# Moving the decoding of weight half-chunks between the stages of an attention and mixture-of-experts kernel

## The chip, the core and the metric

The kernel runs on one core of one Trainium2 chip. The metric is device time in microseconds (us); lower is better. The engines are TensorE (PE in the rows, its weight loads PEld), VectorE (DVE), ScalarE (ACT), GpSimd (POOL) and SyncE (SP), which here only issues DMAs. Each engine takes its instructions in the order in which the program gives them.

## The reference

```python
# 8 batches x 8 heads x 576 positions x 64: causal decayed attention without softmax
attn = ((q @ k.T) / 8 * gamma**(i - j) * (i >= j)) @ v
x = attn as (4608 tokens, 512)
# routing: the 36864 logits x @ w_gate in falling order; a token goes to the first
# of its experts that still has room (576 tokens for each of 8 experts)
for e in range(8):
    out[mask_e] = relu(x[mask_e] @ w1[e]) @ w2[e]        # 512 -> 1024 -> 512
h = out @ w_in                                           # 512 -> 2048
return (h * sigmoid(1.702 * h)) @ w_out                  # 2048 -> 512
```

The weights `w_in` and `w_out` of the last layer come as double precision numbers (8 bytes each), the others as 4-byte floats.

## The kernel before

**Stages.** `build` first runs attention, in 40 iterations (8 batches times 5 blocks of positions). In each it loads blocks ahead, multiplies on TensorE, and puts logits, routing counts and row transposes from the list `fills` in between. Then `R.phase(0, True)` finds the tokens of the first expert, and `ffn` runs the rest. There, `gather(0)` fetches the first expert's 576 rows by five indirect DMAs that GpSimd issues; `prepare` transposes them on TensorE and splits them into a high part `xh` (ScalarE) and a low part `xl` (VectorE), because every product is made of three matmuls (`mm3`). Eight rounds follow. A round is `expert(k)` (w1, then w2, 192 matmuls each) and `block(k)` (the last layer for 512 tokens, 384 matmuls); a ninth block ends the program.

**Decoding.** `w_in` and `w_out` are 16 chunks of 128x1024, and each is decoded in two halves, so there are 32 half-chunks, numbered i. `decode_steps` gives six steps for one of them: s0 loads 512 KB (tile `draw`, SP); s1 is two ScalarE operations (`dr`, `dT`); s2 is two VectorE operations on `dT`; s3 one on VectorE (`dq`); s4 is one VectorE operation, a GpSimd multiplication into `dr` and a GpSimd addition into `dq`; s5 writes `dq` to the array `w32` in DRAM (SP). Blocks read their weights from `w32` later (L456). Before, half-chunks 0 to 17 are decoded in attention, number i at iteration int(2.1 i), with the steps 0, 3, 3, 4, 4 and 6 iterations after it (`AOFF`), and 18 to 31 in the first round.

**Order in the first round.** The program order inside `ffn` is written by a counter of ticks. `tick()` is called after each pair or single of `mm3` groups; it issues what the dictionary `timed` holds for this tick and then one step of the generator `follow(k + 1)`, which does the routing of the next expert (VectorE comparisons `ind`, then counting matmuls on TensorE, line L236 and so on), its gather and its `prepare`. `expert` takes 65 ticks and `block` 128. A half-chunk that starts at tick t has its steps at t + 0, 8, 10, 11, 12 and 14 (`OFF`); number 18 starts at tick 0 and each next one `DSTEP` = 10 ticks later. Because the counting matmuls stand between the block's matmuls in TensorE's queue, they hold TensorE when their `ind` is late.

**Buffers and queues.** In `ffn` a half-chunk uses tiles of the pool `fp` with `FDB` = (2, 2, 1, 2) buffers for `draw`, `dr`, `dT` and `dq`: there is one `dT` buffer, which is free again after the GpSimd multiplication. In attention each has 3. Weight chunks are loaded by `load_to` (SP, tile `raw`, 3 buffers) and split by `split_to` into `wh` (ScalarE) and `wl` (GpSimd or VectorE).

**The start of `ffn`** (L651 to L664):

```python
    warm(WU[0])                  # 9 matmuls without use
    xg = gather(0)
    split_to(2, nc.vector)       # w1 chunks 0 and 1: loads, wh, wl
    load_to(LD)                  # loads of w1 chunks 2 and 3
    rest = prepare(0, xg, True)
    next(rest)
    warm(WU[1])                  # 3 matmuls
    for _ in range(3):
        next(rest)
    for i in range(NDEC, 32):
        for f, o in zip(decode_steps(nc, fp, A, w32, i, 1, nc.vector), OFF):
            timed.setdefault(DSTEP * (i - NDEC) + o, []).append(f)
```

`expert(0)` then takes the transposes of row groups 2, 3 and 4 before its first, second and third matmul group, and asks for the split of w1 chunk 2 before its first group.

Of the kernel before, what the change touches and what calls it, by code (L numbers as in the profile page):

```python
# [25 lines left out]
BIG = 1.5e38  # L26
DEAD = -1.4e38
LAG = 2
NATT, NDEC, DFAST, DSTEP = 18, 18, 14, 10
OFF = (0, 8, 10, 11, 12, 14)  # L30
AOFF = (0, 3, 3, 4, 4, 6)
GD, DB = 1, 3
# [1 line left out]
FDB = (2, 2, 1, 2)  # L34
SL, GW, SW, YW = 1, 8, 2, 1
LGA = 1
X0, XS, XRB = 0, 2.1, 3
PF, XB, GDEF = 5, 3, 30
WU = (9, 3)
AJ = 0  # L40
# [347 lines left out]
def ffn(tc, ctx, A, out, R, xd, w32, idn):  # L388
    nc = tc.nc
    fa = ctx.enter_context(tc.tile_pool(name="first", bufs=1))  # L390
    fp = ctx.enter_context(tc.tile_pool(name="ffn", bufs=1))
# [5 lines left out]
    def gather(k):  # L397
        gi = R.GI[k]
        xg = []
        for g in range(5):  # L400
            w = 128 if g < 4 else 64
            x = fa.tile([128, DM], FT, name="xg", bufs=5)
            nc.gpsimd.indirect_dma_start(out=x[:w], out_offset=None, in_=xd[:],
                                         in_offset=bass.IndirectOffsetOnAxis(ap=gi[:w, g:g + 1], axis=0))
            xg.append(x)
        return xg
# [39 lines left out]
    def load_to(n):  # L446
        while ptr[0] < min(n, len(stream)):
            i = ptr[0]
            kind, k, j = stream[i]
            r = fa.tile([128, 1024], FT, name="raw", bufs=3)  # L450
            if kind[1] in "12":
                if k not in RV:
                    RV[k] = nc.sync.value_load(EI[k][0:1, 0:1], min_val=0, max_val=E - 1)
                nc.sync.dma_start(r, A[kind][ds(RV[k], 1), j].rearrange("e p f -> (e p) f"))
            else:
                nc.sync.dma_start(r, w32[(0 if kind == "wi" else 8) + j])  # L456
            RAW[i] = r
            ptr[0] += 1

    def split_to(n, eng_=None, wait=0):  # L460
        while ptr[1] < min(n, len(stream)):
            i = ptr[1]
            load_to(i + 1)
            r = RAW.pop(i)
            h = fa.tile([128, 1024], FR, name="wh", bufs=4)
            l = fa.tile([128, 1024], FR, name="wl", bufs=4)
            eng = eng_ or nc.gpsimd if stream[i][0] in ("w1", "wi") else nc.vector
            for a in (slice(0, 512), slice(512, 1024)):
                nc.scalar.activation(h[:, a], r[:, a], AF.Copy)  # L469
                f = partial(eng.tensor_tensor, l[:, a], r[:, a], h.bitcast(FT)[:, a], op=OP.subtract)  # L470
                later(wait, f) if wait else f()
            HL[i] = (h, l)
            ptr[1] += 1
# [16 lines left out]
    timed = {}  # L490
    now = [0]

    def later(n, f):
        timed.setdefault(now[0] + n, []).append(f)
# [151 lines left out]
    def warm(n):  # L646
        ps = pp.tile([128, 512], FT, name="po3")
        for _ in range(n):
            nc.tensor.matmul(ps, R.grp, R.zz.rearrange("p a b -> p (a b)"), start=True, stop=True)

    warm(WU[0])  # L651
    xg = gather(0)
    split_to(2, nc.vector)
    if GT is not None:
        nc.sync.dma_start(spacer2, xg[GT][:1, :1])
    load_to(LD)
# [2 lines left out]
    warm(WU[1])  # L659
    for _ in range(3):  # L660
        next(rest)
    for i in range(NDEC, 32):
        for f, o in zip(decode_steps(nc, fp, A, w32, i, 1, nc.vector), OFF):
            timed.setdefault(DSTEP * (i - NDEC) + o, []).append(f)  # L664
    for k in range(E):
        if k + 1 < E:
            gens.append(follow(k + 1))
# [7 lines left out]
def decode_steps(nc, pool, A, w32, i, bufs, eng):  # L675
    j, hf = divmod(i, 2)
    src = A["wi"][j] if j < 8 else A["wo"][j - 8]
    st = {}

    def s0():  # L680
        st["raw"] = pool.tile([128, 512, 2], I32, name="draw", bufs=DB if bufs > 2 else FDB[0])
        nc.sync.dma_start(st["raw"].rearrange("p a b -> p (a b)"), src[:, hf * 512:(hf + 1) * 512].bitcast(I32))

    def s1():
        raw = st["raw"]
        st["r"] = r = pool.tile([128, 512], FT, name="dr", bufs=bufs if bufs > 2 else FDB[1])
        st["T"] = T = pool.tile([128, 512], I32, name="dT", bufs=bufs if bufs > 2 else FDB[2])
        nc.scalar.activation(r, raw[:, :, 0].bitcast(U32), AF.Copy, scale=2.0 ** -52)
        nc.scalar.activation(T.bitcast(FT), raw[:, :, 1].bitcast(FT), AF.Abs)

    def s2():
        T = st["T"]
        nc.vector.tensor_scalar(T.bitcast(FT), T.bitcast(FT), LEAST, None, op0=OP.max)
        nc.vector.tensor_scalar(T, T, 3, 0x3FFFFFF8, op0=OP.logical_shift_left, op1=OP.bitwise_and)

    def s3():
        st["q"] = q = pool.tile([128, 512], FT, name="dq", bufs=bufs if bufs > 2 else FDB[3])
        nc.vector.scalar_tensor_tensor(q.bitcast(I32), st["raw"][:, :, 1], -0x40000000, st["T"], op0=OP.bitwise_and,
                                       op1=OP.bitwise_or)

    def s4():
        q, r, T = st["q"], st["r"], st["T"]
        nc.vector.tensor_scalar(T, q.bitcast(I32), -0x800000, None, op0=OP.bitwise_and)
        nc.gpsimd.tensor_mul(r, r, T.bitcast(FT))
        nc.gpsimd.tensor_add(q, q, r)

    def s5():
        nc.sync.dma_start(w32[j][:, hf * 512:(hf + 1) * 512], st["q"])
    return [s0, s1, s2, s3, s4, s5]


def build(tc, A, out, dbg=None, stop=None):
    nc = tc.nc
# [7 lines left out]
    w32 = dram.tile([16, 128, 1024], FT, name="w32")  # L721
    L = cp.tile([128, NCOL, 8], FT, name="L")
    idn = cp.tile([128, 128], FT, name="idn")
    with ExitStack() as ac:
# [156 lines left out]
        for i in range(NDEC):  # L881
            st = decode_steps(nc, al, A, w32, i, 3, nc.vector)
            if i < NATT:
                x = int(X0 + XS * i)
                for f, o in zip(st, AOFF):
                    sched.setdefault(min(x + o, NCH - 1), []).append(f)
            else:
                sched.setdefault(NCH - 1, []).append(st[0])
                extra.append(st[1:])
# [60 lines left out]
    if dbg and "SI" in dbg:  # L950
        for k in range(1, E):
            for _ in R.phase(k):
                pass
        nc.sync.dma_start(dbg["L"], L)
        nc.sync.dma_start(dbg["SI"], R.SI)
    else:
        ffn(tc, ctx, A, out, R, xd, w32, idn)
# [44 lines left out]
```

## Time and profile before

| what | value |
|---|---|
| median of 3 runs (range) | 1540.36 us (1540.18 to 1540.72) |
| the profiled execution | 1543.02 us |
| its span on the core, first to last instruction | 1541.2 us |
| granted TensorE clock, mean over the span | 0.975 |
| TensorE busy | 1466.0 us (95%) |
| VectorE busy | 863.9 us (56%) |
| GpSimd busy | 714.0 us (46%) |
| ScalarE busy | 610.7 us (40%) |

The profiled execution took 1.8 us more than its span, and 2.7 us more than the median of the three runs. Shares of busy time are means over stages that differ; the stages are attention (to about 191 us of the span), the first routing (to 218 us), the first gather (to 230 us), eight rounds and the last block.

### The profile page before, as it was taken

The page shows a single profiled execution, that of the slowest core. Times are in us where ns is not written, and L with a number is a line of the kernel's source. Part 1 is how long each engine was busy: PE and PEld are TensorE (multiplying, and loading weights), DVE is VectorE, ACT ScalarE, POOL GpSimd, SP SyncE. Part 2 cuts the span into 40 slices and gives each one's busy share as a digit, 9 for nine tenths or more (in the row PEclk, how much of TensorE's full clock was granted, in tenths as well). Part 3 has the DMA queues.
Part 4 walks back from the last instruction along what each step waited for, and adds up shares of the span by engine and source line. Part 5 has one row for each costly group of instructions (what it writes and reads, how often), then busy time and mean ns, then how long its engine had stood idle before and what let it go on. Part 6 is the DMA issues. An engine that isn't in the chain of part 4 may idle for free.

```text
span 1541.2 us, 25721 instructions
## 1 busy us (share of the span) xinstructions
PE 1466.0 (95%) x10031; PEld 1250.3 (81%) x10031; DVE 863.9 (56%) x1759; ACT 610.7 (40%) x1205; POOL 714.0 (46%) x596
## 2 busy tenths in 40 slices
PE   7899869898999999999999999999999999999997
PEld 6788749776897789788978987898789888988885
DVE  4686668787655665566556755575547322332321
ACT  3455414443434443343334333433343434344432
POOL 4766514576415541553245334623462545144643
PEclk9999859999999999999999999999999999999998
DMA  8999444443322432243223322332242333232320
GB/s 326 371 365 385 137 155 141 154 157 135 116 72 94 126 97 83 83 126 110 69 97 114 108 81 98 113 110 83 83 125 99 112 110 100 93 98 93 123 96 28
DMA packets 58858, 202.86 MB, mean 132 GB/s; under 512 B 8304, under 2 KB 8688, under 8 KB 54768
## 3 DMA queue, kind: packets, MB, share of 16 engines
q1 hardware_dynamic: 47008, 171.36, 32.7%
q0 software_dynamic: 5824, 18.88, 3.6%
q10 hardware_dynamic: 5904, 10.98, 1.9%
q8 instruction: 79, 1.29, 0.3%
q14 instruction: 43, 0.35, 0.1%
HBM read 173.93 MB, written 27.26 MB: 131 GB/s over the span
## 4 chain that ended last, share of the span: by engine, by line
PE 70%; DVE 16%; issue 6%; POOL 4%; DMA 2%; ACT 2%; SPq 0%; ACTq 0%; POOLq 0%; DVEq 0%
PE ph L517 14%; PE ph L519 14%; PE ph L518 14%; PE po L517 6%; PE po L518 6%; PE po L519 6%; DVE ind L144 3%; DVE wl L504 3%; PE pR L797 2%; PE pY L819 2%; DVE oh L138 2%; POOL gl L597 2%; PE pY L814 2%; POOL wl L504 1%; DMA qkv<-in_qkv_dram 1%
## 5 line engine op out<-in xcount | busy, mean ns | idle before, releaser
L504 POOL TENSOR_TENSOR wl<-raw,wh 128x512 fp32r<-128x512 f32 x204 | 274.6, 1367 | 238.4 <-ACT wh L469 238.3
L597 POOL TENSOR_TENSOR gl<-g,gh 128x512 fp32r<-128x512 f32 x144 | 204.9, 1423 | 375.4 <-ACT gh L595 371.5
L469 ACT ACTIVATE wh<-raw 128x512 fp32r<-128x512 f32 x416 | 237.6, 622 | 5.2 <-DMA raw<-in_w_dram 5.2
L593 DVE TENSOR_TENSOR g<-ph,sg 128x512 f32<-128x512 f32 x144 | 99.1, 689 | 249.7 <-ACT sg L616 246.4
L517 PE MATMUL po<-wh,gl 128*128 128x512 f32 x576 | 234.2, 407 | 0.8 <-POOL gl L597 0.8
L517 PE MATMUL ph<-yh,wl 128*128 128x512 f32 x576 | 232.9, 404 | 0.0
L518 PE MATMUL po<-wl,gh 128*128 128x512 f32 x576 | 228.5, 397 | 0.0
L519 PE MATMUL ph<-yh,wh 128*128 128x512 f32 x576 | 228.3, 396 | 0.0
L519 PE MATMUL po<-wh,gh 128*128 128x512 f32 x576 | 228.2, 396 | 0.0
L518 PE MATMUL ph<-yl,wh 128*128 128x512 f32 x576 | 226.8, 394 | 0.0
L616 ACT ACTIVATE sg<-ph 128x512 f32<-128x512 f32 x144 | 86.0, 597 | 337.3 <-PE ph L519 321.8
L504 DVE TENSOR_TENSOR wl<-raw,wh 128x512 fp32r<-128x512 f32 x208 | 193.5, 970 | 4.5 <-ACT wh L469 4.0
L517 PE MATMUL ph<-xh,wl 128*128 128x288 f32 (+2 forms) x512 | 154.2, 301 | 7.9 <-DVE hTl L561 3.1
L517 PE MATMUL ph<-hTh,wl 128*128 128x288 f32 x512 | 153.7, 300 | 0.0
L518 PE MATMUL ph<-xl,wh 128*128 128x288 f32 (+2 forms) x512 | 151.3, 296 | 0.0
L519 PE MATMUL ph<-xh,wh 128*128 128x288 f32 (+2 forms) x512 | 151.2, 295 | 0.0
L518 PE MATMUL ph<-hTl,wh 128*128 128x288 f32 x512 | 151.0, 295 | 0.0
L519 PE MATMUL ph<-hTh,wh 128*128 128x288 f32 x512 | 150.7, 294 | 0.0
L519 PEld LDWEIGHTS po<-wh,gh 128*128 128x128 f32 x576 | 108.9, 189 | 26.4
L595 ACT ACTIVATE gh<-g 128x512 fp32r<-128x512 f32 x144 | 90.5, 628 | 99.1 <-DVE g L593 98.9
L517 PEld LDWEIGHTS po<-wh,gl 128*128 128x128 f32 x576 | 109.1, 189 | 24.9 <-POOL gl L597 1.3
L519 PEld LDWEIGHTS ph<-yh,wh 128*128 128x128 f32 x576 | 108.8, 189 | 24.7
(173 smaller groups left out, 2491.7 us busy)
## 6 DMA issues: line engine op xcount, KB each, us to landing
raw<-w SPq DMA_DIRECT2D x144, 512.0 KB, 3.3
raw<-in_w_dram SPq DMA_DIRECT2D x64, 512.0 KB, 3.5
qkv<-in_qkv_dram SPq DMA_DIRECT2D x31, 1024.0 KB, 10.6
xd<-xr ACTq DMA_DIRECT2D x36, 256.0 KB, 6.4
draw<-in_wi_dram SPq DMA_DIRECT2D x16, 512.0 KB, 8.7
w<-dq SPq DMA_DIRECT2D x32, 256.0 KB, 2.5
draw<-in_wo_dram SPq DMA_DIRECT2D x16, 512.0 KB, 5.0
qkt<-in_qkt_dram SPq DMA_DIRECT2D x8, 256.0 KB, 8.0
```

Source lines behind the costliest of these rows:

```text
L138: V.tensor_tensor(oh[:, c0:c1], eq[:, c0:c1], wm[:, c0:c1, None].to_broadcast([128, n, 8]), op=OP.is_equal)
L144: self.nc.vector.tensor_tensor(ind, self.m[:, c0:c1, None].to_broadcast([128, n, T]), cand[:, None, :].to_broadcast([128, n, T]), op=OP.is_ge)
L469: nc.scalar.activation(h[:, a], r[:, a], AF.Copy)
L504: f()
L517: nc.tensor.matmul(ps, al, bh, start=first, stop=False)
L518: nc.tensor.matmul(ps, ah, bl, start=False, stop=False)
L519: nc.tensor.matmul(ps, ah, bh, start=False, stop=last)
L593: nc.vector.tensor_mul(g, ps, sg)
L595: nc.scalar.activation(gh, g, AF.Copy)
L597: nc.gpsimd.tensor_sub(gl, g, gh.bitcast(FT))
L616: nc.scalar.activation(sg, ps, AF.Sigmoid, scale=1.702)
L797: nc.tensor.matmul(p[:w, s, hp, :w], k[s * 64:(s + 1) * 64, hp], q[s * 64:(s + 1) * 64, hp], start=True, stop=True)
```

## The change

Twenty half-chunks instead of 18 are decoded in attention: the first 12 at the iterations they had, the next eight at 25, 26, 28, 29, 30, 32, 33 and 35 (they were six, at 25, 27, 29, 31, 33 and 35). Three (20, 21, 22) are decoded at the start of `ffn`: the loads of the first two stand ahead of the gather, and everything else of the three, the third load and the three writes among it, stands behind the split of w1 chunks 0 and 1 and ahead of the loads of w1 chunks 2 and 3 and of `prepare`. Nine (23 to 31) remain in the first round, 14 ticks apart instead of 10.

```diff
-NATT, NDEC, DFAST, DSTEP = 18, 18, 14, 10
+NATT, NDEC, PRE, DSTEP = 20, 20, 3, 14
-X0, XS, XRB = 0, 2.1, 3
+XS, XT_, XRB = 2.1, 1.4, 3
...
+    pre = [decode_steps(nc, fp, A, w32, i, 1, nc.vector) for i in range(NDEC, NDEC + PRE)]
+    for st in pre[:FDB[0]]:
+        st[0]()
     warm(WU[0])
     xg = gather(0)
     split_to(2, nc.vector)
+    for i, st in enumerate(pre):
+        for f in st[1:]:
+            f()
+        if i + FDB[0] < PRE:
+            pre[i + FDB[0]][0]()
     if GT is not None:
         nc.sync.dma_start(spacer2, xg[GT][:1, :1])
     load_to(LD)
...
-    for i in range(NDEC, 32):
+    for i in range(NDEC + PRE, 32):
         for f, o in zip(decode_steps(nc, fp, A, w32, i, 1, nc.vector), OFF):
-            timed.setdefault(DSTEP * (i - NDEC) + o, []).append(f)
+            timed.setdefault(DSTEP * (i - NDEC - PRE) + o, []).append(f)
...
-                x = int(X0 + XS * i)
+                x = int(XS * i) if i < 12 else int(XS * 12 + XT_ * (i - 12))
```

## Rows read from the trace of the kernel before

**Rows 1.** Busy time by stretch: us, PE, PEld, DVE, ACT, POOL, PE clock, DMA share, GB/s
```profile
230.26:286.81 56.55, 55.32 (x442) 54.38 (x441) 46.74 (x100) 26.11 (x57) 25.06 (x18) 0.98 0.43 145
286.81:402.58 115.77, 102.16 (x478) 79.29 (x477) 87.78 (x137) 50.22 (x90) 75.94 (x57) 0.94 0.42 139
402.58:457.16 54.58, 53.46 (x434) 52.35 (x432) 36.07 (x95) 18.05 (x43) 13.83 (x14) 1.00 0.30 98
457.16:553.58 96.42, 95.39 (x479) 74.71 (x478) 54.23 (x104) 39.99 (x74) 50.19 (x39) 1.00 0.32 100
```

**Rows 2.** Timeline of TensorE, 303 to 372 us: start, duration, instruction [idle before <-releaser]
```profile
307.63 0.29 PE L236 MATMUL pm<-oh,ind 128*128 128x32 f16 x5 [3.81 <-DVE ind L144]
...
338.28 0.27 PE L236 MATMUL pm<-oh,ind 128*128 128x32 f16 x4 [2.28 <-DVE ind L144]
...
354.62 0.19 PE L319 MATMUL pm<-ge,c_tri 128*128 128x72 f16 x1 [2.48 <-DVE ge L310]
...
369.77 0.45 PE L351 MATMUL pm<-hv,ind 128*128 128x36 f16 x9 [2.96 <-DVE ind L345]
```

**Rows 3.** The same timeline, matmuls before and after the first of these stops
```profile
303.07 0.39 PE L518 MATMUL po<-wl,gh 128*128 128x512 f32 x1
...
308.70 0.63 PE L519 MATMUL po<-wh,gh 128*128 128x512 f32 x1
```

**Rows 4.** Instructions on the decode's tiles, whole span: duration ns min/median/max, first and last start
```profile
L689 ACT ACTIVATE dT<-draw x32: 641/665/705, 27.0 to 357.7; 128x512 f32<-128x512 f32 x32
L693 DVE TENSOR_SCALAR dT<-dT x32: 408/429/1502, 27.7 to 358.4; 128x512 f32<-128x512 f32 x32
L694 DVE TENSOR_SCALAR dT<-dT x32: 426/632/1409, 29.0 to 360.0; 128x512 int32<-128x512 int32 x32
L698 DVE SCALAR_TENSOR_TENSOR dq<-draw,dT x32: 674/691/1742, 32.3 to 361.4; 128x512 int32<-128x512 int32 x32
L703 DVE TENSOR_SCALAR dT<-dq x32: 411/426/1399, 33.1 to 363.3; 128x512 int32<-128x512 int32 x32
L704 POOL TENSOR_TENSOR dr<-dr,dT x32: 1264/1280/1702, 33.6 to 363.8; 128x512 f32<-128x512 f32 x32
L705 POOL TENSOR_TENSOR dq<-dq,dr x32: 1259/1284/1680, 35.0 to 365.2; 128x512 f32<-128x512 f32 x32
```

**Rows 5.** Timeline of VectorE, 328 to 404 us
```profile
328.21 0.90 DVE L693 TENSOR_SCALAR dT<-dT 128x512 f32<-128x512 f32 x1 [1.29 <-ACT dT L689]
...
347.55 1.43 DVE L693 TENSOR_SCALAR dT<-dT 128x512 f32<-128x512 f32 x1
...
351.17 0.43 DVE L703 TENSOR_SCALAR dT<-dq 128x512 int32<-128x512 int32 x1
...
358.42 1.50 DVE L693 TENSOR_SCALAR dT<-dT 128x512 f32<-128x512 f32 x1
```

**Rows 6.** Timelines of GpSimd, VectorE and TensorE at the first gather
```profile
218.79 1.42 POOL L403 DMA_INDIRECT xg<-xd,gi  x1 [3.76 <-DMA raw<-in_w_dram]
...
224.53 0.90 POOL L403 DMA_INDIRECT xg<-xd,gi  x1 [0.30 <-issue]
...
219.61 2.49 DVE L471 TENSOR_TENSOR wl<-raw,wh 128x512 fp32r<-128x512 f32 x4
...
229.50 1.11 PE L420 MATMUL ph<-idn,xg 128*128 128x128 f32 x4 [2.19 <-DMA xg<-xd,gi]
...
234.90 0.46 PE L420 MATMUL ph<-idn,xg 64*128 64x64 f32 x4
```

**Rows 7.** DMA issues of the page: count, KB each, median us from issue to landing
```profile
raw<-in_w_dram SPq DMA_DIRECT2D x64, 512.0 KB, 3.5
...
draw<-in_wo_dram SPq DMA_DIRECT2D x16, 512.0 KB, 5.0
```

**Rows 8.** Busy time by stretch in attention, columns as in rows 1
```profile
124.20:143.10 18.90, 18.90 (x286) 16.63 (x285) 12.60 (x21) 10.95 (x22) 12.10 (x10) 1.00 1.02 395
143.10:152.80 9.70, 8.21 (x130) 6.85 (x128) 8.71 (x13) 6.01 (x13) 7.40 (x6) 1.00 1.02 387
```

## The prediction

> **What bounds the kernel now.** I read the busy time by stretch first, cut at the first matmul of each expert and block. In the second round an expert takes 54.58 us and a block 96.42 us, with TensorE busy for nearly all of it: there the kernel is bound by its matmuls [rows 1]. In the first round, the one that decodes, the expert takes 56.55 us, but the block takes 115.77 us. These 19.35 us are all that decoding can be costing there, and the bound of what this change can win in the block. VectorE is busy 87.78 us in that block against 54.23 us in the next, GpSimd 75.94 against 50.19.
>
> TensorE is idle for 115.77 - 102.16 = 13.61 us of that block [rows 1]. Its timeline has four long stops, each before a matmul of the next expert's routing that waits for VectorE: A ends at 307.63 us (3.81 us), B at 338.28 us (2.28 us), C at 354.62 us (2.48 us) and D at 369.77 us (2.96 us), 11.53 us together [rows 2]; 2.1 us are in smaller ones. After a stop matmuls of the same shape are slower for some microseconds, 0.63 us for one instead of 0.39 us, and the granted clock over the block is 0.94, against 1.00 in the next: TensorE falls for a while from 2.4 to 1.2 GHz [rows 1, 3]. What idle time does not explain, 19.35 - 13.61 = 5.74 us, I share among the four stops: 1.43 us each.
>
> The gather is another stage. The first matmul of `expert(0)` at 230.26 us comes right behind the transposes of row group 2, which waited for their rows [rows 1, 6]. VectorE, ScalarE and GpSimd have little to do there, but what they do is in series.
>
> **Part 1, the first round.** One half-chunk costs, by the medians, 2 x 0.67 us of ScalarE, 0.43 + 0.63 + 0.69 + 0.43 = 2.18 us of VectorE and 1.28 + 1.28 = 2.56 us of GpSimd [rows 4]. Beside busy GpSimd it is more: the half-chunk at 347.55 us holds VectorE until 351.60 us, 4.05 us [rows 5]. With the block beginning at tick 65, half-chunks had their VectorE steps at ticks 70, 80, ... 140, eight of them in the block; now at 66, 80, 94, 108 and 122, five. Stop by stop:
>
> - C and D come right behind the half-chunks of ticks 130 and 140 (347.55 and 358.42 us), which stand in front of the routing's operations in VectorE's queue [rows 5]. None has its VectorE steps after tick 124 now. Both stops go: 2.48 + 2.96 + 2 x 1.43 = 8.3 us.
> - B comes behind the half-chunk of tick 110, which begins only at 328.21 us, 10 us ahead of the stop's end, because ScalarE was late with it [rows 5]. Its successor is two ticks earlier (about 1.5 us), and the half-chunk of tick 100 ahead of it is gone. I take the stop as gone: 2.28 + 1.43 = 3.7 us. At the other end it stays.
> - A has a half-chunk at tick 80 before and after. I let it stay (0); at the other end it goes too, 3.81 + 1.43 = 5.25 us, because the GpSimd work of the preceding half-chunk now ends some four ticks earlier.
> - Of the 2.1 us in smaller stops I take half, 1.0 us; the ends are none and all.
>
> Sum: 8.3 + 3.7 + 1.0 = 13.0 us won; the ends are 8.3 us and, with A, 18.3 us. In `expert(0)` I win nothing: it is only 2 us above the next expert, and that is its start at the low clock. The decoded weights are on time: the last write moves from tick 144 to tick 126, and the load that needs it is issued at tick 153.
>
> **Part 2, the gather.** Here I follow every queue, because three half-chunks are put in front of `prepare` on ScalarE, VectorE and SP, and behind the five gathers on GpSimd.
>
> - The loads of 20 and 21 go to SP early. Their tiles lie where attention's last operands lay, free at about 191 us; they land long before use. No cost.
> - GpSimd is through with the gathers at 224.53 + 0.90 = 225.43 us [rows 6]. Only then comes the multiplication of 20 (to 226.7 us), then its addition (to 228.0 us). There is one `dT` buffer, so ScalarE's second operation for 21 waits until 226.7 us, and everything of `prepare` on ScalarE waits behind it.
> - On SP the write of 20 waits until 228.0 us, and the load of 22 stands behind it: issued at about 228.5 us. It lands after 3.5 us (weight loads) to 5.0 us (half-chunk loads) [rows 7]: 232.0 to 233.5 us. Half-chunk 21 is through with VectorE at 229.6 us and has freed `dT` at 230.9 us, so this load is what comes last.
> - ScalarE then does 22 (1.35 us), VectorE 22 (2.18 us), and only then the two `xl` that the first matmul needs (0.62 us each, as the four like operations of 2.49 us) [rows 4, 6]. The first matmul comes at 236.8 to 238.3 us instead of 230.26: 6.5 to 8.1 us late.
> - That is not all. The addition of 22 ends at 238.1 to 239.7 us; SP writes it, and only then loads w1 chunk 2: landed 0.7 + 3.5 us later, at 242.3 to 243.9 us. ScalarE has the split of that chunk ahead of the first `hTh`, so the PSUM buffer that row group 4's transposes need comes free only after the split, `hTh`, `xh`, `xl` and `hTl`, some 3 us: 245.3 to 246.9 us, against 234.90 us [rows 6].
>
> The loss is 10.4 to 12.0 us; I take 11.2 us. TensorE stands idle some 3 us more on the way, which may cost part of another 1.45 us at the low clock; I add 0.7 us. Ends: 6.5 us, if the second delay hides in the buffers, and 13.5 us.
>
> By the Trainium skill's page "SBUF — State Buffer", section "SBUF: two separate sides", VectorE and GpSimd share a port pair that one of them locks for a whole instruction, so that VectorE can hold up the descriptors of a DMA that GpSimd issues. The trace has something like it: a gather's issue takes 1.42 us with VectorE's `wl` work beside it, and 0.90 us without [rows 6]. By the rule the decode operations of 20, at 222 to 224.4 us, would stretch up to three more issues by 0.5 us, and all of the above would come 1.5 us later; the sum does without it.
>
> **Part 3, attention.** Eight half-chunks in iterations 25 to 35 instead of six. From 124.20 to 143.10 us TensorE has no idle time at all and VectorE is busy 12.60 of 18.90 us, so one more of 2.18 to 4.05 us fits beside it [rows 5, 8]. From 143.10 to 152.80 us it is the other way: VectorE is busy 8.71 of 9.70 us and TensorE idle for 1.49 us behind it [rows 8]. There the count of the third pair of batches waits behind decode operations, and the new spacing puts the shorter pair (s3, s4) where the longer (s2) was. DMAs move 395 GB/s with their queues full; two more half-chunks add 2 x 768 KB, 4 us of transfer, while blocks are loaded five iterations ahead. I take +0.5 us, ends -1.5 us (that wait goes) and +8.1 us (both half-chunks in the path at 4.05 us each). If VectorE's free time were not there, that upper end is the price.
>
> **Sum.** -13.0 + 11.2 + 0.7 + 0.5 = -0.6 us. The profiled execution of 1543.02 us (span 1541.2 us) would become 1542.4 us; it lies 2.66 us above the median of the runs, so in their terms 1540.36 - 0.6 = 1539.8 us.
>
> **Rivals.**
> - *Only C and D go* (slower). B's cause has moved by two ticks only. Then -8.3 + 12.4 = +4.1 us, 1544.5 us. It decides as soon as the block gives back less than the 12 us that the gather takes. For it: eight half-chunks become five, and 5/8 of the loss would even leave 12.1 us. Against it: VectorE stood idle for 1.29 us just before tick 110's half-chunk [rows 5], so its queue was not yet late. 0.20.
> - *Attention pays in full* (slower): +7.6 us more, 1547.4 us. The gapless stretch speaks against it. 0.04.
> - *A goes too* (faster): -5.25 us, 1534.5 us. For it: GpSimd and VectorE lengthen one another's operations at A, and one of GpSimd's half-chunks leaves that spot. 0.23.
> - *The second delay of the gather hides* (faster): w1 chunk 2 would come in time, or the start be only 6.5 us late: -5.4 us, 1534.4 us. Against it: the order on SP and ScalarE is fixed. 0.13.
> - *VectorE holds up the gathers* (the port rule above): +1.5 us, 1541.3 us. The trace shows such a stretch on two issues of five. 0.04.
>
> **Numbers.** The forecast keeps 0.36. About 0.2% (3.1 us) is what a measurement of this kernel can tell from no change. Faster by more: 0.23 + 0.13 = 0.36; within: 0.36 + 0.04 = 0.40; slower: 0.20 + 0.04 = 0.24. The forecast's own range, with part of each end, is 1536 to 1543 us; for 8 in 10 it has to reach past the faster cases at 1534.4 us and the slower one at 1544.5 us: 1532.5 to 1546 us.
>
> **What would show it.** The first w1 matmul 6.5 to 8 us later than its old place behind the first routing, ScalarE waiting for the load of 22 and then for w1 chunk 2; the transposes of row group 4 some 11 us late; the first block near 103 us, with no stop at its routing's end; attention's end unmoved within 1 us. The prediction is wrong if `prepare` is not held up (then the kernel is 10 us faster), or if the block stays above 107 us.

## The result, and the profile after

The changed kernel is slower: 1560.71 us median (1558.85 to 1561.19, 4 runs) against 1540.54 us (1540.18 to 1541.47, 4 runs) of the kernel before, a ratio of 1.0126 (95% interval 1.0112 to 1.0140). The forecast was 1539.8 us, with a range up to 1546. Its profiled execution took 1558.85 us, with a span of 1557.1 us, 15.9 us more than the span before; the stages below are taken from these two. The medians are 20.2 us apart, because this execution was the fastest of its four and the one profiled before, at 1543.02 us, slower than all four of its kernel. In the changed kernel every line from `build` on has a number that is 8 higher.

I cut both traces at five places: the end of the cast that gives the first gather its indices (`gi`, L366), the transposes of row group 4, the first matmul of w2, the first matmul of the first block, and the first matmul of the second round. The pieces add up to the span.

| stage | before, us | after, us | difference | forecast |
|---|---|---|---|---|
| start to `gi` (attention, first routing) | 217.94 | 224.79 | +6.85 | +0.5 |
| `gi` to the transposes of row group 4 | 16.96 | 28.65 | +11.69 | +11.2 |
| from there to w2 | 25.22 | 28.84 | +3.62 | +0.7 |
| w2 | 26.69 | 27.61 | +0.92 | 0 |
| first block | 115.77 | 108.80 | -6.97 | -13.0 |
| everything behind it | 1138.64 | 1138.38 | -0.26 | 0 |

So the forecast for the gather was right to half a microsecond, and three others were wrong. Busy time by stretch in the changed kernel: the start of w1, the rest of w1, w2, and the first block (columns as in [rows 1], which it answers to).

```profile
244.28:253.44 9.16, 6.36 (x28) 5.92 (x28) 1.79 (x4) 2.18 (x5) 3.93 (x4) 0.68 0.70 229
253.44:282.29 28.85, 26.35 (x191) 25.67 (x191) 25.32 (x50) 10.96 (x24) 9.19 (x7) 0.92 0.38 111
282.29:309.90 27.61, 27.61 (x223) 27.24 (x223) 16.99 (x43) 9.98 (x23) 10.22 (x8) 0.96 0.42 130
309.90:418.70 108.80, 98.47 (x479) 76.19 (x477) 68.90 (x121) 47.31 (x85) 62.37 (x50) 0.97 0.39 128
```

VectorE has 18.9 us less to do in the block than in [rows 1], and TensorE is still idle for 108.80 - 98.47 = 10.33 us. The timeline of TensorE shows one long stop where there were four [rows 2]:

```profile
328.64 0.29 PE L236 MATMUL pm<-oh,ind 128*128 128x32 f16 x5 [1.65 <-DVE ind L144]
...
347.37 0.29 PE L236 MATMUL pm<-oh,ind 128*128 128x32 f16 x4 [5.53 <-DVE ind L144]
...
372.35 0.17 PE L256 MATMUL pm<-sc,c_wt 128*128 128x8 bf16 x1 [1.70 <-DVE sc L250]
```

The long stop isn't one of the four. The counting matmuls of L236 come four times in the block: before, A stood at the second time and B at the fourth. Now A is the 1.65 us of the first row, and the 5.53 us stand at the third time, which before had next to nothing (TensorE's timeline of the kernel before):

```profile
322.84 0.29 PE L236 MATMUL pm<-oh,ind 128*128 128x32 f16 x5 [0.35 <-DVE ind L144]
```

At the fourth time there is no stop any more; B, C and D are gone (the changed kernel):

```profile
363.06 0.39 PE L236 MATMUL pm<-oh,ind 128*128 128x32 f16 x9
```

What the 5.53 us waited for is seen by going back through three queues. SP's timeline:

```profile
332.43 0.32 SPq L716 DMA_DIRECT2D w<-dq  x1
332.80 0.42 SPq L690 DMA_DIRECT2D draw<-in_wo_dram  x1
```

ScalarE's:

```profile
338.08 0.66 ACT L696 ACTIVATE dr<-draw 128x512 f32<-128x512 uint32 x1 [6.13 <-DMA draw<-in_wo_dram]
```

VectorE's:

```profile
339.33 0.43 DVE L701 TENSOR_SCALAR dT<-dT 128x512 f32<-128x512 f32 x1 [6.58 <-ACT dT L697]
```

Read upwards: VectorE stands idle for 6.58 us for ScalarE, ScalarE 6.13 us for a half-chunk's load, and SP issued this load only at 332.80 us, right behind the write of the half-chunk before it, which had waited for GpSimd's addition. With 14 ticks between half-chunks, the write of one (its step at tick 14) and the load of the next (tick 0) fall on the same tick, and the write stands first in the list. Before, with 10 ticks, the load stood four ticks ahead of the write.

The gather shows the chain that was forecast (the rows answer to [rows 6]). The timeline of GpSimd, the last gather and the first half-chunk:

```profile
231.70 0.91 POOL L403 DMA_INDIRECT xg<-xd,gi  x1 [0.30 <-issue]
233.15 1.26 POOL L712 TENSOR_TENSOR dr<-dr,dT 128x512 f32<-128x512 f32 x1 [0.55 <-PE ph L420]
```

ScalarE, which waits for GpSimd, for the load of half-chunk 22 and for w1 chunk 2:

```profile
234.44 0.67 ACT L697 ACTIVATE dT<-draw 128x512 f32<-128x512 f32 x1 [3.12 <-POOL dr L712]
240.22 0.66 ACT L696 ACTIVATE dr<-draw 128x512 f32<-128x512 uint32 x1 [5.11 <-DMA draw<-in_wo_dram]
...
250.76 1.15 ACT L469 ACTIVATE wh<-raw 128x512 fp32r<-128x512 f32 x2 [7.87 <-DMA raw<-in_w_dram]
```

SP, whose load of half-chunk 22 (236.22 us) stands behind one write, and that of w1 chunk 2 (246.86 us) behind two more:

```profile
220.32 0.81 SPq L690 DMA_DIRECT2D draw<-in_wo_dram  x2
222.21 0.91 SPq L454 DMA_DIRECT2D raw<-in_w_dram  x2
235.79 0.33 SPq L716 DMA_DIRECT2D w<-dq  x1
236.22 0.37 SPq L690 DMA_DIRECT2D draw<-in_wo_dram  x1
...
246.86 1.53 SPq L454 DMA_DIRECT2D raw<-in_w_dram  x3
```

TensorE, the first w1 matmul and the transposes of row group 4:

```profile
244.28 0.55 PE L517 MATMUL ph<-xh,wl 128*128 128x256 f32 x1 [10.87 <-DVE xl L424]
...
253.44 0.61 PE L420 MATMUL ph<-idn,xg 64*128 64x64 f32 x4 [2.80 <-DVE xl L424]
```

In attention the longer time stands in two stops ahead of the counting matmuls. TensorE's timeline, the stops of 1 us and more between 140 and 192 us:

```profile
154.86 0.40 PE L156 MATMUL pm<-oh,ind 128*128 128x8 f16 x9 [4.57 <-DVE ind L144]
171.50 0.23 PE L156 MATMUL pm<-oh,ind 128*128 128x8 f16 x3 [1.12 <-DVE ind L144]
189.71 0.24 PE L156 MATMUL pm<-oh,ind 128*128 128x8 f16 x3 [4.60 <-DVE ind L144]
```

The first and the last of them are 5.4 us longer together than before, of the 6.85 us. Before, the three were 1.49, 1.35 and 2.27 us (the first and the last, in the timeline of the kernel before):

```profile
152.52 0.38 PE L156 MATMUL pm<-oh,ind 128*128 128x8 f16 x9 [1.49 <-DVE ind L144]
...
183.79 0.23 PE L156 MATMUL pm<-oh,ind 128*128 128x8 f16 x3 [2.27 <-DVE ind L144]
```

The changed kernel's timeline of VectorE ahead of the first of them:

```profile
140.40 1.29 DVE L808 TENSOR_TENSOR R<-pR,dk 128x512 f32<-128x512 f32 x2 [1.94 <-PE pR L805]
...
143.11 1.38 DVE L702 TENSOR_SCALAR dT<-dT 128x512 int32<-128x512 int32 x1
144.42 1.27 DVE L808 TENSOR_TENSOR R<-pR,dk 128x512 f32<-128x512 f32 x2
...
147.22 1.38 DVE L711 TENSOR_SCALAR dT<-dq 128x512 int32<-128x512 int32 x1
...
152.38 2.42 DVE L144 TENSOR_TENSOR ind<-m,c_pat 128x1152 f16<-128x1152 f32 x1
```

and of GpSimd:

```profile
142.89 1.32 POOL L712 TENSOR_TENSOR dr<-dr,dT 128x512 f32<-128x512 f32 x1 [2.31 <-DVE dT L711]
144.29 1.34 POOL L713 TENSOR_TENSOR dq<-dq,dr 128x512 f32<-128x512 f32 x1
...
146.60 1.72 POOL L794 TENSOR_TENSOR qs<-qkv,qd 128x512 f32<-128x512 f32 x1
```

The `dT` operation that begins at 143.11 us ends at 144.49 us, 0.28 us behind the GpSimd multiplication that began before it (142.89 + 1.32 = 144.21 us); alone it takes 0.43 us. The comparison `ind` takes 2.42 us; in the kernel before it took 1.34 us (its timeline of VectorE):

```profile
151.12 1.34 DVE L144 TENSOR_TENSOR ind<-m,c_pat 128x1152 f16<-128x1152 f32 x1
```

### The profile page after: what moved, and what is told of

It reads as the page before. It is cut to its first block, busy times and chain, and to the rows that moved or that the text cites. A ratio compares the mean times of both kernels' runs of the same rounds, so it can differ in the third digit from the quotient of the medians.

```text
span 1557.1 us, 25729 instructions
## 1 busy us (share of the span) xinstructions
PE 1470.9 (94%) x10031; PEld 1254.8 (81%) x10031; DVE 858.7 (55%) x1759; ACT 610.5 (39%) x1205; POOL 712.8 (46%) x596
## 3 DMA queue, kind: packets, MB, share of 16 engines
q8 instruction: 79, 1.29, 0.3%
## 4 chain that ended last, share of the span: by engine, by line
PE 74%; DVE 14%; DMA 4%; issue 3%; ACT 2%; POOL 2%; SPq 0%; ACTq 0%; DVEq 0%; POOLq 0%
PE ph L517 15%; PE ph L519 14%; PE ph L518 14%; PE po L517 7%; PE po L519 7%; PE po L518 7%; DVE ind L144 3%; DVE wl L504 3%; DMA draw<-in_wo_dram 2%; PE pR L805 2%; PE pY L827 2%; DVE oh L138 2%; PE pY L822 2%; DMA qkv<-in_qkv_dram 1%; PE pm L420 1%
## 5 line engine op out<-in xcount | busy, mean ns | idle before, releaser
L504 DVE TENSOR_TENSOR wl<-raw,wh 128x512 fp32r<-128x512 f32 x208 | 189.5, 951 | 4.2 <-ACT wh L469 3.7
L517 PE MATMUL ph<-xh,wl 128*128 128x288 f32 (+2 forms) x512 | 155.8, 304 | 20.1 <-DVE xl L424 10.9
L517 PEld LDWEIGHTS ph<-yh,wl 128*128 128x128 f32 x576 | 109.0, 189 | 23.2 <-issue 1.8
```

Of the source, the lines that this page charges most:

```text
L517: nc.tensor.matmul(ps, al, bh, start=first, stop=False)
```

## The experiments

My theory after the result: three causes that don't depend on one another, the write ahead of the load, the gather, and attention's VectorE beside GpSimd, while C and D went as forecast. The first four kernels take the change apart, the next four test what is behind each part, the last four try to keep the gain without the costs. Diffs are against the changed kernel, and every ratio is to the kernel before on the same chip (medians of 1540.88, 1540.35 and 1540.46 us for the three groups).

| kernel | median, us | ratio, 95% interval | to `gi` | gather | to w2 | block 0 |
|---|---|---|---|---|---|---|
| before (profile shown) | | | 217.94 | 16.96 | 25.22 | 115.77 |
| changed | 1560.71 | 1.0126 [1.0112, 1.0140] | 224.79 | 28.65 | 28.84 | 108.80 |
| 1 write one tick later | 1550.03 | 1.0056 [1.0037, 1.0076] | 223.82 | 28.91 | 28.32 | 102.10 |
| 2 gather part alone | 1545.85 | 1.0030 [1.0018, 1.0041] | 216.65 | 29.47 | 26.31 | 107.00 |
| 3 attention part alone | 1540.95 | 1.0001 [0.9990, 1.0012] | 221.93 | 16.87 | 25.24 | 107.56 |
| 4 two at the gather | 1558.99 | 1.0124 [1.0098, 1.0151] | 224.41 | 23.38 | 28.05 | 116.01 |
| 5 two, attention as before | 1532.63 | 0.9955 [0.9941, 0.9969] | 213.41 | 19.93 | 24.47 | 107.46 |
| 6 the same at 8 ticks | 1539.12 | 0.9991 [0.9981, 1.0002] | 215.25 | 19.84 | 27.94 | 109.13 |
| 7 w1 loads first | 1554.55 | 1.0086 [1.0070, 1.0102] | 223.74 | 26.03 | 29.86 | 107.62 |
| 8 attention, less GpSimd | 1527.33 | 0.9914 [0.9896, 0.9933] | 209.23 | 17.72 | 25.22 | 107.82 |
| 9 as 5, attention early | 1533.27 | 0.9958 [0.9944, 0.9972] | 214.98 | 19.66 | 25.24 | 107.48 |
| 10 twenty evenly | 1535.00 | 0.9970 [0.9960, 0.9980] | 219.40 | 17.72 | 24.07 | 106.83 |
| 11 twenty early | 1534.69 | 0.9969 [0.9958, 0.9980] | 218.34 | 16.65 | 25.24 | 107.58 |
| 12 the change mended | 1540.60 | 1.0008 [0.9998, 1.0017] | 219.12 | 25.35 | 27.10 | 102.02 |

The last four columns are stages of one profiled execution each, in us, cut as in the table above ("gather" is from `gi` to the transposes of row group 4). w2 takes 26.7 us in all but the changed kernel and number 6 (27.6), and what follows block 0 takes 1138.4 to 1138.8 us in all. Up to `gi` the kernel before and numbers 2, 5 and 6 decode the same 18 half-chunks at the same iterations, and still differ by 4.5 us (213.41 to 217.94); so a smaller difference between two single executions in that column shows nothing.

**1. The write one tick later.**

```diff
-OFF = (0, 8, 10, 11, 12, 14)
+OFF = (0, 8, 10, 11, 12, 15)
```

> The changed kernel with one number different: in the first round the write of a half-chunk comes 15 ticks after its load, not 14, so that with half-chunks 14 ticks apart the next load stands in front of the write on SP, and not right behind it. Theory 1 (the loads are held on SP behind writes that wait for GpSimd, and ScalarE then waits for them): ScalarE's waits for half-chunk loads in the first round go (2.9, 6.1 and 1.6 us in the changed kernel), the stop of 5.53 us in the first block falls to 2 us or less and the stop of 2.48 us in w1 goes; the first block falls from 108.8 to about 101 us, the whole to about 1549 us. Rival (VectorE and GpSimd are simply too full there): within 2 us of the changed kernel, 1560 us, with the stops in place.

It gained 10.7 us by the medians; of the 8.8 us between the two profiled spans 6.7 are in the block, which fell to 102.10 us. Now a load of the next half-chunk is issued 8 us ahead of the write that it used to follow (SP's timeline):

```profile
320.54 0.42 SPq L690 DMA_DIRECT2D draw<-in_wo_dram  x1
328.54 0.32 SPq L716 DMA_DIRECT2D w<-dq  x1
```

The stop of 5.53 us is one of 1.27 us (TensorE's timeline); that of 2.48 us in w1, which I had expected to go, is still one of 1.59 us:

```profile
339.22 0.27 PE L236 MATMUL pm<-oh,ind 128*128 128x32 f16 x4 [1.27 <-DVE ind L144]
```

The order on SP was the cause of what the block lacked: it now gives back 115.77 - 102.10 = 13.7 us, against 13.0 in the forecast, though not by the same terms (see the account of part 1 below).

**2, 3 and 4. The parts of the change.** Number 2 has three half-chunks at the gather and attention as before; number 3 has 20 in attention and none at the gather; both go on at 10 ticks. Number 4 is the changed kernel with two instead of three at the gather, so ten in the round.

```diff
-NATT, NDEC, PRE, DSTEP = 20, 20, 3, 14
+NATT, NDEC, PRE, DSTEP = 18, 18, 3, 10    # number 2, with XT_ = 2.1
+NATT, NDEC, PRE, DSTEP = 20, 20, 0, 10    # number 3
+NATT, NDEC, PRE, DSTEP = 20, 20, 2, 14    # number 4
```

> Only the gather part: attention as before (18 half-chunks, 2.1 iterations apart), three at the start of the first round's setup, 11 in the round 10 ticks apart as before. Theory 1: the gather costs 11 to 12 us up to the transposes of row group 4, as in the changed kernel, and some 2 us more at the low clock; the block wins 8 us because nothing is decoded after tick 114: about 1545 us. Rival (the gather costs more than the chain of waits, because what follows in the expert is disturbed as well): expert 38 us for w1 as in the changed kernel, 1550 us or more.

> Only the attention part: 20 half-chunks in attention with the changed spacing, none at the gather, 12 in the first round 10 ticks apart as before. Theory 1: attention ends 6 to 7 us late as in the changed kernel (two stops of 4.6 us before counting matmuls), the gather takes no longer than before, the block wins about 8 us (no half-chunk has its VectorE steps after tick 122): 1538 to 1540 us. Rival (attention's loss in the changed kernel's profile is one execution's accident): attention within 1 us of before, about 1532 us.

> The changed kernel with two half-chunks at the gather instead of three, ten in the first round 14 ticks apart. Theory 1: no load stands behind a write at the gather, so the first w1 matmul comes about 6 us earlier than in the changed kernel and the load of w1 chunk 2 some 7 us earlier; the tenth half-chunk in the round costs 1 to 3 us: about 1555 us. Rival (each half-chunk at the gather costs its work, a third of the loss): 3 to 4 us earlier, minus the tenth: 1559 us.

Numbers 2 and 3 agree with the theory in the main. Each takes the half-chunks behind tick 124 away, and in each the block falls by 8.8 and 8.2 us: C and D are gone, A (3.83 and 3.64 us) and B (2.30 and 2.28 us) are there. That is the 8.3 us at which I had put C and D. The gather costs 12.5 us alone (29.47 - 16.96). Attention's part costs 4.0 us by this one profile, less than the 6 to 7 that I had expected; but number 3's median is that of the kernel before (I had expected 1538 to 1540 us), so over its runs attention must cost about the 8.2 us that the block gives back. Number 4's time was the rival's, but not by its mechanism: the gather did become 5.3 us shorter, as the theory said, while the tenth half-chunk of the round, with its VectorE work at tick 136, brought D back (3.75 us), beside a stop of 5.08 us where the changed kernel has its 5.53, and the block took 116.01 us.

**5 and 6. Two at the gather, attention untouched.** The loads of w1 chunks 2 and 3 (`load_to`) are also put ahead of the half-chunks' steps. Number 6 has 8 ticks in place of 10.

```diff
-NATT, NDEC, PRE, DSTEP = 20, 20, 3, 14
+NATT, NDEC, PRE, DSTEP = 18, 18, 2, 10    # number 6: 18, 18, 2, 8
-XS, XT_, XRB = 2.1, 1.4, 3
+XS, XT_, XRB = 2.1, 2.1, 3
...
     split_to(2, nc.vector)
+    load_to(LD)
     for i, st in enumerate(pre):
```

> Attention is left as in the kernel before (18 half-chunks there), two half-chunks instead of three are decoded at the first gather, twelve follow in the round at 10 ticks, so that a load stands 4 ticks ahead of the write of the half-chunk before it, and the loads of the first w1 chunk are issued ahead of the half-chunks' steps. Theory (a load held behind a write, a longer gather and a longer attention are the three costs of the change, and stops C and D the gain): attention as before, the gather about 1 us longer (only ScalarE's table for the second half-chunk waits there), C and D gone from the first block (about -8 us), A and B left: 1532 to 1534 us. Rival (two at the gather cost what three cost): about 1543 us.

> The same with 8 ticks from one half-chunk to the next instead of 10. A half-chunk's load then stands at tick 8 of the one before, still 6 ticks ahead of that one's write. If stop B comes from late half-chunks beside the block, it goes as well: about 1529 us. Rival (VectorE has no room for a half-chunk in every 8 ticks): new stops in w1, w2 and the early block, and a time above the 10-tick version's.

Number 5 beats both kernels. Two half-chunks need no third load behind a write, and with the w1 loads first the gather is 19.93 us (23.38 in number 4, which has two without that; 3.0 more than before, where I had expected 1), and the block gives 8.3 us back. TensorE's timeline, to be held against the changed kernel's 10.87 and 2.80 us:

```profile
227.73 0.55 PE L517 MATMUL ph<-xh,wl 128*128 128x256 f32 x1 [4.17 <-DVE xl L424]
...
233.34 0.46 PE L420 MATMUL ph<-idn,xg 64*128 64x64 f32 x4
```

At 8 ticks B does go, as I had expected (the fourth counting has no stop), but the kernel is 6.5 us slower than number 5: the way to w2 is 3.5 us longer, w2 0.9 us and the block 1.7 us. A grows from 3.81 to 4.56 us, and the first and the third counting get stops of 1.18 and 1.20 us. That fits the rival (VectorE has no room); which wait begins these stops was not followed further.

**7. The w1 loads first, in the changed kernel.**

```diff
     split_to(2, nc.vector)
+    load_to(LD)
     for i, st in enumerate(pre):
```

> The changed kernel whole, with the loads of the first w1 chunk issued ahead of the three half-chunks' steps instead of behind them. If the second delay of the gather (the second w1 chunk's load waiting behind the write of the third half-chunk) is what makes the transposes of row group 4 late, they come some 4 us earlier against the first w1 matmul and the kernel gains 3 to 4 us on the changed one: about 1557 us. Rival (the transposes wait for something else, such as the third half-chunk's table on ScalarE): no change, 1560 us.

The transposes of row group 4 come 5.86 us behind the first w1 matmul instead of 9.16, so this second delay is 3.3 us of the gather's 11.7, and its cause is the w1 load behind the half-chunks' writes. The first matmul itself comes no earlier (20.17 us behind `gi`, after 19.49): it hangs on the load of half-chunk 22. The kernel gained 6.2 us by the medians, more than this delay and more than the 3 to 4 us that I had expected; the profile puts the rest in attention (1.05), w2 (0.9) and the block (1.2), less 1.0 us on the way to w2. I had no reason for those and take none from it.

**8. Attention with less GpSimd.** Number 3 without the GpSimd operations of half-chunks 12 to 19, whose weights are then not finished:

```diff
-        nc.gpsimd.tensor_mul(r, r, T.bitcast(FT))
-        nc.gpsimd.tensor_add(q, q, r)
+        if not 12 <= i < 20:
+            nc.gpsimd.tensor_mul(r, r, T.bitcast(FT))
+            nc.gpsimd.tensor_add(q, q, r)
```

> The attention part alone (20 half-chunks in attention, 10 ticks, none at the gather) with GpSimd's multiply and addition left out of half-chunks 12 to 19; the weights that these decode are therefore wrong, and the output isn't the reference's. If VectorE's operations late in attention are stretched by GpSimd's, they shrink to what they take elsewhere, the two long stops ahead of the counting matmuls come back to the size that they had before (1.5 and 2.3 us) and the first routing ends 4 us or more earlier than with GpSimd's work (221.9 us). Rival (it is VectorE's own added operations and their order): the stops stay at 4.6 and 6 us and the routing ends at 221 to 222 us.

`gi` comes 12.7 us earlier than in number 3, and the two stops shrink from 4.58 to 0.80 us and from 6.18 to 1.29 us. VectorE has the same instructions in both kernels. Its groups by line and form between 140 and 205 us (busy us, mean ns), first in number 3:

```profile
L702 DVE TENSOR_SCALAR dT<-dT 128x512 int32<-128x512 int32 x7 | 7.8, 1109 | 0.2
L701 DVE TENSOR_SCALAR dT<-dT 128x512 f32<-128x512 f32 x7 | 5.2, 743 | 0.2 <-ACT dT L697 0.2
L711 DVE TENSOR_SCALAR dT<-dq 128x512 int32<-128x512 int32 x8 | 5.1, 637 | 0.3
L144 DVE TENSOR_TENSOR ind<-m,c_pat 128x1152 f16<-128x1152 f32 x1 | 2.4, 2422 | 0.0
```

and then in number 8:

```profile
L702 DVE TENSOR_SCALAR dT<-dT 128x512 int32<-128x512 int32 x7 | 4.8, 684 | 0.2
L711 DVE TENSOR_SCALAR dT<-dq 128x512 int32<-128x512 int32 x8 | 4.1, 518 | 0.3
L701 DVE TENSOR_SCALAR dT<-dT 128x512 f32<-128x512 f32 x7 | 3.5, 503 | 0.0
L144 DVE TENSOR_TENSOR ind<-m,c_pat 128x1152 f16<-128x1152 f32 x1 | 1.3, 1344 | 0.0
```

It is GpSimd's work that makes VectorE's late, and with it the counting matmuls.

**9 to 12. Where the half-chunks stand in attention, and the change mended.** Number 9 is number 5 with a half-chunk every 1.8 iterations, numbers 10 and 11 are number 3 with one every 1.85 and 1.6. Number 12 is the changed kernel with the edits of numbers 1 and 7 and one every 1.85.

```diff
-XS, XT_, XRB = 2.1, 1.4, 3
+XS, XT_, XRB = 1.85, 1.85, 3     # number 9: 1.8, number 11: 1.6
```

> The version with two at the gather and 10 ticks, its 18 half-chunks of attention now one every 1.8 iterations instead of every 2.1, so that the last load stands at iteration 30 instead of 35. Theory (a half-chunk is dear only late in attention, where the routing's work is on VectorE and its operations are stretched beside GpSimd's): the stops of 1.5 to 2.3 us ahead of the counting matmuls shrink and the first routing ends 3 to 6 us earlier: 1527 to 1530 us. Rival (a half-chunk costs the same wherever it stands, or the early loads slow the transfers that attention itself waits for): 1533 us or more.

> The attention part alone with its 20 half-chunks spread evenly, one every 1.85 iterations, so that the last loads stand at iterations 31, 33 and 35 as in the kernel before, instead of seven within eleven iterations. Theory (it is the crowding late in attention that costs, not the two more): attention ends within 2 us of the kernel before, C and D stay gone: 1532 to 1535 us. Rival (two more half-chunks cost 4 to 6 us wherever they stand): 1539 to 1541 us.

> The same with one half-chunk every 1.6 iterations, so that the last load stands at iteration 30. Theory: attention ends earlier than in the kernel before by some 3 us, and the kernel takes 1527 to 1531 us with nothing decoded at the gather. Rival (the loads, more of them in each stretch, slow the transfers on which attention waits: the DMA engines are 0.94 to 1.00 busy there): 1540 us or more, with new stops early in attention.

> The changed kernel with three places mended at once: the write one tick later, the loads of the first w1 chunk ahead of the three half-chunks' steps, and the 20 half-chunks spread evenly over attention. If the three causes add up, it gains on the changed kernel 10.7 (the write) + some 5 (the w1 loads) + some 5 (attention): 1540 us. Rival (they overlap, since each uncovers the next wait): 1545 us or more.

Spread evenly, twenty cost less: `gi` at 219.40 and 219.12 us in numbers 10 and 12, against 221.93 to 224.79 us in the five crowded ones, with stops of 2.20 and 2.29 us in number 10 where number 3 has 4.58 and 6.18. The ratios say the same more surely: 0.9970 in number 10, 1.0001 in number 3. That is what I expected of number 10 (1535.00 us), and it is faster than before with nothing decoded at the gather. Earlier than that brings nothing more: numbers 9 and 11 failed what I expected of them (no 3 to 6 us; 1533.27 and 1534.69 us), and an earlier stop grew, near 110 us, from 2.27 (number 5) to 3.08 us (number 9). Number 12 came out at 1540.60 us, as expected: by the medians it gains 20.1 us, nearly the sum of the three mends alone (10.7, 6.2, and 6.0 from number 3 to number 10). The change is then no faster and no slower than the kernel before, because this first block (busy time by stretch)

```profile
298.26:400.28 102.02, 97.41 (x479) 75.83 (x478) 71.54 (x121) 46.15 (x83) 62.78 (x50) 0.98 0.38 129
```

is paid for by the gather and the way to w2 behind it.

## Why the prediction was wrong, step by step

Between the two profiled spans the sum of -0.6 us missed by 16.5 us: 6.4 in attention, 6.0 in the block, 3.8 behind the gather.

- **Part 1, the block (forecast -13.0, measured -7.0 us): the path was wrong.** I followed VectorE's ticks and never SP's queue in the round. The load and the write that share a tick cost what is missing; with the write one tick later the block gives 13.7 us. C and D were right: numbers 2, 3 and 5, in which A and B stay, measure them alone as 8.8, 8.2 and 8.3 us (forecast 8.3). B was right as well: at 14 ticks it is gone, and the 5.53 us stand at another counting. A, which I let stay, was not: it fell from 3.81 to 1.65 us (1.50 to 1.72 in the kernels with 14 ticks, 3.64 to 3.83 in those with 10). That 13.7 us come so near to 13.0 is therefore partly luck: in number 1 A gives 2.3 us that I had not counted, and stops of 1.27 and 1.43 us that I had not seen coming (at the third counting and at L256) take about as much back.
- **Part 2, the gather (forecast +11.2, measured +11.7 us): right, by the forecast chain.** Number 7 shows its second delay apart (3.3 us). One sentence was wrong: the loads of 20 and 21 did not go early. They stand at 220.32 us, not near 191 us, and SP's row in the summed waits from 195 to 252 us says why:

```profile
SPq L690 <- DMA xd<-xr: 24.6, 1, 24.6
```

  Before they could be issued, the last row write of attention had to land, and the w1 loads queued behind them (222.21 us; before, at 212.77 us). This cost little: GpSimd comes to half-chunk 20 only after the gathers, and stood idle for 0.55 us ahead of it (its row at 233.15 us).
- **The low clock behind the gather (forecast +0.7, measured +3.6 in the rest of w1 and +0.9 in w2): a stop was missing.** The granted clock is 0.68 from 244.28 to 253.44 us and 0.92 in the rest of w1 (before 0.73 and 1.00), and there is a stop that I had not seen coming. VectorE's timeline:

```profile
275.50 2.38 DVE L504 TENSOR_TENSOR wl<-raw,wh 128x512 fp32r<-128x512 f32 x2
277.81 1.61 DVE L144 TENSOR_TENSOR ind<-m,c_pat 128x384 f16<-128x384 f32 x1
```

  GpSimd's:

```profile
275.73 1.61 POOL L712 TENSOR_TENSOR dr<-dr,dT 128x512 f32<-128x512 f32 x1 [9.79 <-ACT hTh L560]
277.42 1.59 POOL L713 TENSOR_TENSOR dq<-dq,dr 128x512 f32<-128x512 f32 x1
```

  TensorE's:

```profile
279.81 0.41 PE L517 MATMUL ph<-xh,wl 128*128 128x320 f32 x1 [2.48 <-DVE hTl L561]
```

  The second half-chunk of the round (24) falls on w1, whose `wl`, `ind` and `hTl` wait on VectorE while GpSimd works; the `ind` of 1.61 us takes 0.54 us at 279.68 us. Its load, too, stood on SP right behind a write (266.40 after 265.97 us). Number 2 tells the stop and the clock apart: after as late a gather, at a granted clock of 0.68 and then 0.89, it takes 26.32 us in the rest of w1 with TensorE never idle, 1.1 us more than before, and nothing more in w2. The changed kernel is busy for 26.35 us there and idle for 2.50. So the clock costs about 1.1 us, near to the forecast, and the stop 2.5 us; the 0.9 us of w2 follow the stop, at a granted clock of 0.96 (1.00 in number 2).
- **Part 3, attention (forecast +0.5, measured +6.9 us): mis-sized.** This was the rival to which I gave 0.04, and its price (+8.1 us) was the right one; the stretch without gaps, for which I had put it aside, was no ground against it. Over the profiles shown, `gi` ends at 213.41 to 217.94 us in the four kernels with 18 half-chunks at their old places (mean 215.8) and at 221.93 to 224.79 us in the five with 20 crowded (mean 223.7), 7.9 us apart. I had taken VectorE's free time, 6.3 of 18.9 us [rows 8], as room for another half-chunk. It was not room: VectorE's operations there are lengthened by GpSimd's beside them (number 8), so each half-chunk adds VectorE time to others too, and the counting matmuls stand behind all of it.
- **The rivals.** "Only C and D go" was right only for 10 ticks. "A goes too" was right for more than half of A at 14 ticks, and could not be seen in the time. "The second delay of the gather hides" did not come: the transposes of row group 4 stand 9.16 us behind the first w1 matmul, before 4.64. "VectorE holds up the gathers" hardly happened: the five issues end 7.8 us after `gi`, before 7.5.

## What to carry to other kernels

When steps of different work items share a tick or an iteration, write out the order on each in-order DMA queue: a load behind a write that waits for an engine is late by that engine's lag, and here such a pair undid half of the gain. Don't count an engine's idle share as room when another engine lengthens its operations: measure the operation beside that other engine's work, and spread the items before adding more. The fastest of the kernels that finish all weights gives the gather just two half-chunks, whose steps need no transfer in between, and leaves attention alone (number 5: 1532.63 us, 0.9955 of before; number 9, at 0.9958, can't be told from it).

## What the runs showed of the hardware that I had not expected

Some VectorE operations that begin while GpSimd runs an elementwise operation do not share with it, but end a little after it: 1.38 us in place of 0.43 us at 143.11 us, 0.28 us behind the end of GpSimd's multiplication; the same at 147.22 us, 0.28 us behind the end of L794 (146.60 + 1.72 = 148.32 us); and 1.61 in place of 0.54 us at 277.81 us, 0.41 us behind the end of its addition (277.42 + 1.59 = 279.01 us). Not all do: the two of L808 at 144.42 us, which read a matmul's output (`pR`), begin beside GpSimd's addition (144.29 to 145.63 us) and take 1.27 us, no more than the 1.29 us at 140.40 us, where GpSimd was idle for most of the time. The Trainium skill's page "SBUF — State Buffer", section "SBUF: two separate sides", states that the port pair which these two engines share goes to one of them for a whole instruction; these rows and number 8 agree with it. In the prediction I had set this rule against the gathers alone, where it did little; its place was attention.
